# Attention of two blocks first, then the gate and value products of both blocks per weight chunk

## The chip, the cores and the metric

The kernel runs on one core of a Trainium2 chip. The core has a matrix engine (TensorE, PE in the profile; its weight loads are PEld), VectorE (DVE), ScalarE (ACT), GpSimd (POOL) and SyncE (SP), which here only issues transfers. Each engine works through its own instructions in order and waits for the others through semaphores. The metric is the time of one execution on the device in microseconds.

## The reference

Three stages, one behind the other: attention over keys and values averaged in groups of 8, a gated layer (4608 tokens, 512 to 1536 to 512), and a second layer with ELU (512 to 2048 to 512).

```python
k_p = k.reshape(B, H, Sp, pool, D).mean(axis=3)
v_p = v.reshape(B, H, Sp, pool, D).mean(axis=3)
scores = scale * np.matmul(q, k_p.transpose(0, 1, 3, 2))
attn = softmax(scores)                      # 72 keys per head
x = np.matmul(attn, v_p)                    # 8 batches of 576 tokens, 8 heads of 64
gate = 1.0 / (1.0 + np.exp(-(x @ w_gate)))
val = x @ w_val
x = gate * val @ w_out
h = x @ w_in
out = np.where(h > 0.0, h, np.exp(np.minimum(h, 0.0)) - 1.0) @ w_out2
```

The weights arrive as 64-bit floats, two 32-bit words for each number.

## The kernel before, in words

The 4608 tokens are worked in 12 blocks of 384, each of three tiles of 128. A block of 384 tokens may reach over two batches of 576: blocks 0 and 2 lie in one batch, block 1 in two. Every matrix product is made of three passes of single-precision matmuls: each operand is kept as a high part (a copy that ScalarE rounds) and a low part (the difference, on GpSimd or VectorE), and `PASSES` multiplies high by high, high by low and low by high. `split` makes both parts.

**Weights.** The gated layer's hidden size of 1536 is cut in `C1` = 12 chunks of 128. For each chunk three tiles must be converted from 64-bit words: gate, value and output weights, 36 jobs in all. One call of `convert` works on VectorE (L106, L110, L116, L120: clamp, shift and two merges), with a magnitude on ScalarE (L188) one job ahead, and ends with the split of the job before: high part on ScalarE, low part on GpSimd (both by the helper at L93 and L94). The raw words come through two buffers `raw` and, for most even jobs up to job 30, through places of the output weights that are still free; jobs 29 and 31 to 35 go through the two `raw` buffers alone. SyncE issues all loads in program order.

**Attention of a block.** Keys of a batch: five tiles are summed on VectorE (`pool_k`, L354), transposed on TensorE, and copied by ScalarE and VectorE into `kbd` (`emit_k`). Values: `pool_v` (L373, L375) and `place_v` on GpSimd (L384), which fills ten rotating buffers `vbd`. Per tile of queries: `emit_q` transposes, `emit_s` makes the scores (L414) and on VectorE their maximum and difference (L422, L425), `emit_exp` the exponential on ScalarE, `emit_norm` the sums on VectorE (L436 to L438) and the product on GpSimd (L439), `emit_t` the transposes (L454) and their split into `pt`. `emit_pv` multiplies `pt` with the values and splits the result into `x`. One PSUM buffer of two banks, `at`, serves keys, queries, scores, transposes and half of the value products in turn.

**Gated layer of a block.** For each chunk: gate product (12 matmuls, L501, into one of two banks `gv`), sigmoid on ScalarE (L509), value product (12 matmuls), sigmoid times value on VectorE (L513), split into `g`; one chunk later the output product (12 matmuls, L520) adds to four banks `acc`. Behind the last chunk `flush_y` copies these to row tiles and stores them.

**Order.** The order of the program is written out by hand. Ahead of the first chunk, block 0's attention is made and five jobs are converted. In block 0 each chunk holds three calls of `convert`: one between sigmoid and value product, one behind the value product, one behind the split of `g`. Attention of block n+1 is spread over the chunks of block n by `plan`. From block 1 on, `prepare` takes 20 steps per block of the 170 that make the second layer's weights. The second layer starts behind block 11.

Of the kernel before, what the change touches and what calls it, by code (L numbers as in the profile page):

```python
# [24 lines left out]
def fused_kernel(  # L25
# [22 lines left out]

    nc = tc.nc
# [28 lines left out]
    y_dram = [dram.tile([P, KD, NB], F32, name=f"yd{i}", tag=f"yd{i}") for i in range(NBLK)]  # L78
    w_dram = [dram.tile([P, 2, 7, 256], F32, name=f"wd{i}", tag=f"wd{i}") for i in range(C2 // 2)]
# [362 lines left out]
    def emit_t(t, spare=False):  # L442
        n, i = divmod(t, TPB)
        if i == 0:
            pt[n] = at_p.tile([P, 2, NCH, NB], F32R, name="pt", tag="pt")
# [9 lines left out]
        for m, c0, c1, src in (  # L455
# [3 lines left out]
            hi = pt[n][:m, 0, c0:c1, i * P:(i + 1) * P]  # L459
            lo = pt[n][:m, 1, c0:c1, i * P:(i + 1) * P]  # L460
# [5 lines left out]
    def emit_pv(n):  # L466

        p = pt.pop(n)
        x = act.tile([P, 2, KD, NB], F32R, name="x", tag="x")
# [6 lines left out]
        for o, w, b, s in segs(n * NB, NB):  # L476
            for j in range(HP):
                for e in range(2):
                    vb, m = v_bd[b, j, e]
                    for a_w, a_p in PASSES:  # L480
# [3 lines left out]
                            rhs=p[:m, a_p, j + e, o:o + w],  # L484
# [120 lines left out]
    with tc.manual_schedule():  # L605
# [3 lines left out]
        def spare(name):  # L609
            return wts.tile([P, 4, 512], F32, name=name, tag="wg", bufs=C1)  # L610

        k0, q0, qt0, p0, v0, q1, k1, v1 = [
            spare(x) for x in ("k0", "q0", "qt0", "p0", "v0", "q1", "k1", "v1")
        ]
        l0, l1 = [wts.tile([P, 2, 512], F32, name=x, tag="wo", bufs=C1) for x in ("l0", "l1")]
        fetch_to(1)
        load_all("k", 0, k0, l0[:, 0])
        fetch_to(2)
        for i in range(TPB):
            load_q(i, q0[:, i])  # L620
        fetch_to(3)
        load_all("v", 0, v0, l0[:, 1])
        fetch_to(4)
# [14 lines left out]
        convert(1, 1, 0)  # L638
# [3 lines left out]
        open_to(2)  # L642
        for i in range(TPB):
            emit_q(i, qt0[:, i])
        convert(1, 2)
        ph = p0.rearrange("p a n -> p (a n)")
        ph = [ph[:, i * HK:(i + 1) * HK] for i in range(TPB)]
        emit_exp(emit_s(0, ph[0]))
        emit_exp(emit_s(1, ph[1]))
        emit_norm(0, ph[0])  # L650
        convert(1, 2)
        emit_exp(emit_s(2, ph[2]))
        emit_norm(1, ph[1])
        emit_t(0, True)
        for c in range(NCH):
            pool_v(0, c)
        emit_norm(2, ph[2])
        place_v(0, 0)
        place_v(0, 1)
        emit_t(1, True)  # L660
        convert(1, 2)
        place_v(0, 2)
        place_v(0, 3)
        emit_t(2, True)
        for i in range(TPB):
            load_q(TPB + i, q1[:, i])
# [89 lines left out]
        for n in range(NBLK):  # L756
# [3 lines left out]
            for c in range(C1):  # L760
# [16 lines left out]
                elif c in QUIET:  # L777
                    prepare()
# [236 lines left out]
```

## Time and profile before

| | us |
|---|---|
| median of 3 runs | 1940.83 (1938.94 to 1941.63) |
| the profiled execution | 1936.11 |
| its span, first to last instruction | 1934.1 |
| TensorE busy | 1839.1 (95%) |
| VectorE busy | 922.0 (48%) |
| ScalarE busy | 795.1 (41%) |
| GpSimd busy | 510.6 (26%) |

Times within the span count from its first instruction. In a line of the timeline the first number is the start, the second the duration; a part in brackets is the time for which the engine was idle before it and what ended that. `x12` is a number of instructions merged into one line.

### The profile page before, as it was taken

The numbers are of one execution on the slowest core, as the hardware profiler recorded it, in microseconds if no ns is written. First come the engines' busy times: TensorE is split into PE (matmuls) and PEld (weight loads), VectorE is DVE, ScalarE is ACT, GpSimd is POOL, SyncE is SP. The second block draws the span as 40 slices with busy tenths as digits, with TensorE's granted clock in tenths as the row PEclk, the third lists the DMA queues.
The fourth block names the chain that finished last, engine by engine and source line by source line (L and its number), as shares of the span: only waits on it lengthen the run. The fifth ranks groups of instructions, "written<-read, shape, count | busy, mean of one in ns | idle before, by whom it ended". The sixth has DMA issues, their size and how long they took to land.

```text
span 1934.1 us, 25810 instructions
## 1 busy us (share of the span) xinstructions
PE 1839.1 (95%) x9996; PEld 1730.7 (89%) x9996; DVE 922.0 (48%) x1531; ACT 795.1 (41%) x1499; POOL 510.6 (26%) x523
## 2 busy tenths in 40 slices
PE   3776999999999999999999998999999999999999
PEld 3665999999999999999999997898989899999997
DVE  7997455554445554555532133443444344443422
ACT  3543334333333333443333223454454444544543
POOL 4454222222213122223222112222222222222222
PEclk7888999999999999999999999999999999999999
DMA  7332123232223322232310324334353343344330
GB/s 221 110 128 80 50 90 106 76 99 71 85 77 90 128 69 82 96 110 80 104 28 1 137 97 188 117 137 159 120 189 124 125 182 115 145 149 147 153 115 33
DMA packets 115771, 213.49 MB, mean 110 GB/s; under 512 B 43968, under 2 KB 72640, under 8 KB 115648
## 3 DMA queue, kind: packets, MB, share of 16 engines
q1 hardware_dynamic: 115648, 211.84, 32.1%
q8 instruction: 78, 1.28, 0.3%
q14 instruction: 45, 0.37, 0.1%
HBM read 169.87 MB, written 41.94 MB: 110 GB/s over the span
## 4 chain that ended last, share of the span: by engine, by line
PE 85%; DVE 9%; ACT 2%; DMA 2%; issue 1%; POOL 0%; SPq 0%; DVEq 0%; ACTq 0%; POOLq 0%
PE gv L501 27%; PE oacc L896 20%; PE bank L850 18%; PE acc L520 13%; PE xv L481 2%; PE atv L481 2%; PE ats L414 2%; DVE ks L354 2%; DVE nt L106 1%; DVE nt L116 1%; DVE nt L120 1%; PE atq L404 1%; PE att L454 1%; ACT L509 1%; DMA rkv<-in_k_dram 1%
## 5 line engine op out<-in xcount | busy, mean ns | idle before, releaser
L501 PE MATMUL gv<-x,wg 128*128 128x384 f32 x3456 | 654.1, 342 | 22.9 <-DVE sg L513 19.6
L501 PEld LDWEIGHTS gv<-x,wg 128*128 128x128 f32 x3456 | 608.5, 191 | 29.4 <-ACT wo L93 14.1
L896 PE MATMUL oacc<-w2o,gc 128*128 128x512 f32 x1728 | 454.5, 394 | 4.8 <-ACT yo L537 2.4
L896 PEld LDWEIGHTS oacc<-w2o,gc 128*128 128x128 f32 x1728 | 319.9, 188 | 54.5 <-DVE yo L535 3.2
L850 PE MATMUL bank<-form,wr 128*128 128x384 f32 x1728 | 354.0, 339 | 1.9 <-DVE ea L863 1.4
L94 POOL TENSOR_TENSOR g<-sg,g 128x384 fp32r<-128x384 f32 x144 | 156.1, 1084 | 720.6 <-ACT g L93 720.6
L850 PEld LDWEIGHTS bank<-form,wr 128*128 128x128 f32 x1728 | 315.3, 188 | 25.7 <-DVE ea L863 1.7
L520 PE MATMUL acc<-g,wo 128*128 128x384 f32 x1728 | 328.0, 336 | 2.9 <-POOL g L94 2.9
L520 PEld LDWEIGHTS acc<-g,wo 128*128 128x128 f32 x1728 | 302.6, 189 | 6.6 <-POOL g L94 4.5
L513 DVE TENSOR_TENSOR sg<-sg,gv 128x384 f32<-128x384 f32 x144 | 79.2, 550 | 328.0 <-PE gv L501 328.0
L94 POOL TENSOR_TENSOR gc<-ea,gc 128x384 fp32r<-128x384 f32 x96 | 98.1, 1022 | 299.3 <-ACT gc L93 296.2
L94 POOL TENSOR_TENSOR gc<-eb,gc 128x384 fp32r<-128x384 f32 x96 | 98.0, 1020 | 267.3 <-ACT gc L93 245.3
L509 ACT ACTIVATE sg<-gv 128x384 f32<-128x384 f32 x144 | 70.7, 491 | 226.5 <-PE gv L501 226.0
L93 ACT ACTIVATE g<-sg 128x384 fp32r<-128x384 f32 x144 | 75.6, 525 | 176.8 <-DVE sg L513 176.6
L859 ACT ACTIVATE ea<-bank 128x384 f32<-128x384 f32 x48 | 23.6, 492 | 157.6 <-PE bank L850 157.6
L863 DVE SCALAR_TENSOR_TENSOR ea<-ea,bank 128x384 f32<-128x384 f32 x48 | 26.6, 555 | 116.6 <-ACT ea L860 116.6
L94 DVE TENSOR_TENSOR pt<-att,pt 128x512 fp32r<-128x512 f32 x72 | 34.8, 486 | 99.3 <-ACT pt L93 99.2
L859 ACT ACTIVATE eb<-c 128x384 f32<-128x384 f32 x48 | 25.2, 525 | 129.3 <-DVE c L880 129.3
L874 DVE TENSOR_TENSOR u<-p,bank 128x384 f32<-128x384 f32 x48 | 26.6, 555 | 99.0 <-PE bank L850 96.8
L93 ACT ACTIVATE gc<-eb 128x384 fp32r<-128x384 f32 x96 | 50.4, 525 | 56.8 <-DVE eb L863 33.0
L93 ACT ACTIVATE gc<-ea 128x384 fp32r<-128x384 f32 x96 | 50.5, 526 | 55.4 <-DVE ea L863 55.4
L509 ACT ACT_TABLE_LOAD x34 | 43.6, 1283 | 66.5 <-PE gv L501 66.3
(104 smaller groups left out, 1885.3 us busy)
## 6 DMA issues: line engine op xcount, KB each, us to landing
wr<-wd SPq DMA_DIRECT2D x96, 896.0 KB, 6.3
rw<-in_moe_w_out_dram SPq DMA_DIRECT2D x23, 512.0 KB, 3.6
yd<-yo SPq DMA_DIRECT2D x48, 192.0 KB, 2.1
r<-yd SPq DMA_DIRECT2D x24, 384.0 KB, 7.6
out_dram<-po SPq DMA_DIRECT2D x36, 256.0 KB, 2.0
rw<-in_moe_w_in_dram SPq DMA_DIRECT2D x16, 512.0 KB, 4.4
wd<-rw SPq DMA_DIRECT2D x16, 512.0 KB, 3.4
wod<-rw SPq DMA_DIRECT2D x16, 512.0 KB, 2.8
```

Source lines behind the costliest of these rows:

```text
L93: nc.scalar.activation(out=dst_hi, in_=src, func=AF.Copy)
L94: eng.tensor_tensor(out=dst_lo, in0=src, in1=f32(dst_hi), op=ALU.subtract)
L354: nc.vector.tensor_reduce(out=t[:n, 0], in_=r.rearrange("p (r d) -> p d r", r=POOL), op=ALU.add, axis=AX.X)
L414: nc.tensor.matmul(a[o:o + n, j // 2, (j % 2) * w:(j % 2 + 1) * w], lhsT=qt[:, j * P + o:j * P + o + n], rhs=kbd[b % 2][:, j * w:(j + 1) * w],
L481: nc.tensor.matmul(d[j][:, o:o + w], lhsT=vb[:m, a_w].rearrange("p e d -> p (e d)"), rhs=p[:m, a_p, j + e, o:o + w], start=(e == 0 and a_w ...
L501: nc.tensor.matmul(d, lhsT=w[:, i, a_w, j], rhs=x[:, a_x, j], start=(j == 0 and a_w == 0 and a_x == 0), stop=(j == KD - 1 and a_w == 1),)
L509: nc.scalar.activation(out=sg, in_=gps, func=AF.Sigmoid)
L513: nc.vector.tensor_tensor(out=sg, in0=sg, in1=vps, op=ALU.mult)
L520: return lambda: nc.tensor.matmul(acc[m], lhsT=wo[c][:, a_w, m * P:(m + 1) * P], rhs=g[:, a_g], start=(c == 0 and a_w == 0 and a_g == 0), ...
L850: nc.tensor.matmul(bank[b ^ flip], lhsT=wp[q][a_w][:, w, j * P:(j + 1) * P], rhs=form_tile(s, a)[j][:, a_x], start=opens and n == 0, stop= ...
L859: nc.scalar.activation(out=e, in_=src, func=AF.Relu, scale=-1.0)
L896: return lambda: nc.tensor.matmul(acc[t + i], lhsT=g[c][:, a_g, i * P:(i + 1) * P], rhs=wo2[2 * q + e][:, a_w], start=opens and p == 0, st ...
```

## The change

The first two blocks are treated by themselves. The attention of both comes ahead of the first chunk, with the same five conversions between the tiles of block 1. Then one loop over the 12 chunks makes, per chunk, block 0's gate and value products with three conversions, block 0's output product of the chunk before, and the gate and value products of block 1 for the chunk before. Block 1's sigmoid times value is not split but stored to HBM (`g_dram`). Behind the loop block 1's 12 output products are made from these stored tiles, among the attention of block 2. From block 2 on the loop is the one of before, and the steps of `prepare` begin there. The second layer's first two output banks are taken from `gv`, the other four from `acc`.

```diff
+        def keep_g(c):
+            sg = emit_sig(emit_gate(x1, c, 0))
+            vps = emit_gate(x1, c, 1)
+            def rest():
+                nc.vector.tensor_tensor(out=sg, in0=sg, in1=vps, op=ALU.mult)
+                nc.sync.dma_start(out=g_dram[c], in_=sg)
+            return rest
...
+        for c in range(C1):
+            gps = emit_gate(x0, c, 0)
+            sg = emit_sig(gps)
+            if rest:
+                rest()
+            convert(1)
+            vps = emit_gate(x0, c, 1)
+            convert(1)
+            g = emit_g(sg, vps)
+            convert(1)
+            last_y()
+            if c == 0:
+                acc = outputs()
+            pend = (0, acc, g, c)
+            if c > 0:
+                rest = keep_g(c - 1)
+        rest()
+        keep_g(C1 - 1)()
+        do(("ldq", 2 * TPB))
...
+        def second_y(n):
+            nonlocal done, pend
+            for _ in range(n):
+                if done < C1:
+                    g = act.tile([P, 2, NB], F32R, name="g", tag="g", bufs=2)
+                    split(g[:, 0], g[:, 1], g_raw.pop(done))
+                    load_g(done + 2)
+                if pend:
+                    last_y()
+                pend = (1, acc, g, done)
+                done += 1
+        for i in range(TPB):
+            t = 2 * TPB + i
+            do(("q", t))
+            second_y(1)
+            scores = emit_s(t)
+            emit_exp(scores)
+            second_y(1)
+            emit_norm(t, scores)
+            second_y(2)
+            do(("ldq", t + 1))
+            if i == 1:
+                for c in range(3):
+                    do(("lk", 2, c))
+            do(("t", t))
+            if i == 2:
+                for c in range(3, NCH):
+                    do(("lk", 2, c))
+                for c in range(NCH):
+                    do(("pk", 2, c))
+        do(("k", 2))
+        emit_pv(2)
-        for n in range(NBLK):
+        for n in range(2, NBLK):
...
-                            ps.tile([P, DM], F32, name="oacc", tag="acc" if i < 4 else "gv", bufs=4 if i < 4 else 2)
+                            ps.tile([P, DM], F32, name="oacc", tag="gv" if i < 2 else "acc", bufs=2 if i < 2 else 4)
```

The part ahead of the loop:

```diff
+        for t in range(2 * TPB):
+            emit_exp(emit_s(t, ph[t]))
+            if t > 1:
+                emit_t(t - 2, True)
+            between(t)
+            emit_norm(t, ph[t])
+            if t > 2:
+                convert(1, 2)
+        for t in range(2 * TPB - 2, 2 * TPB):
+            emit_t(t, True)
+            convert(1, 2)
+        emit_pv(1)
```

`between` holds block 1's keys and queries (t = 0 and 1), batch 0's values and their placement (2 and 3), and batch 1's values with the first two placements and block 0's value products (4).

TensorE, two chunks in the middle of block 0. Before, a chunk is gate and value products with one weight chunk (`wg_...`), then the output product of the chunk before, with parts of block 1's attention between:

```order
L501 MATMUL gv<-x,wg_826 128x384 x12
L454 MATMUL att<-ident,p 128x128 x4
L454 MATMUL att<-ident,p 64x128
L501 MATMUL gv<-x,wg_826 128x384 x12
L520 MATMUL acc<-g,wo_811 128x384 x12
```

The same two places in the changed kernel; `wg_699` and `wg_767` belong to neighbouring chunks:

```order
L507 MATMUL gv<-x,wg_767 128x384 x24
L526 MATMUL acc<-g,wo_752 128x384 x12
L507 MATMUL gv<-x,wg_699 128x384 x24
L507 MATMUL gv<-x,wg_873 128x384 x24
L526 MATMUL acc<-g,wo_858 128x384 x12
```

A chunk has grown from 36 products to 60, the last 24 of them block 1's with the weights of the chunk before, and no attention stands between them.

VectorE in one chunk of the changed kernel's loop; L519 is block 0's sigmoid times value, L793 block 1's, the groups of four one conversion each:

```order
L519 TENSOR_TENSOR sg<-sg,gv 128x384
L118 SCALAR_TENSOR_TENSOR nt<-rw,nt 128x512
L108 TENSOR_SCALAR nt<-nt 128x512
L122 SCALAR_TENSOR_TENSOR nt<-rw,nt 128x512
L112 TENSOR_SCALAR nt<-nt 128x512
L793 TENSOR_TENSOR sg<-sg,gv 128x384
L118 SCALAR_TENSOR_TENSOR nt<-rwo,nt 128x512
L108 TENSOR_SCALAR nt<-nt 128x512
L122 SCALAR_TENSOR_TENSOR nt<-rwo,nt 128x512
L112 TENSOR_SCALAR nt<-nt 128x512
```

Before, the place of L793 held parts of block 1's attention (key and value sums, scores, probabilities).

SyncE behind the loop, with the loads of the kept products (`rg<-gd`), of queries (`rq`) and of keys (`rkv`):

```order
L319 DMA rq<-in_q_dram 128x8x64
L801 DMA rg<-gd_83 128x384
L801 DMA rg<-gd_84 128x384
L544 DMA yd_71<-yo 128x384 x4
L801 DMA rg<-gd_85 128x384
L801 DMA rg<-gd_86 128x384
L801 DMA rg<-gd_87 128x384
L801 DMA rg<-gd_88 128x384
L319 DMA rq<-in_q_dram 128x8x64
```

All of these but the query loads and the stores of `yo` are new; each query load stands behind the loads of kept products that the program issues before it, and each of those needs one of the two `raw` buffers free.

## Rows read from the trace of the kernel before

**Rows 1.** Page, busy tenths of TensorE in 40 equal slices of the span

```profile
PE   3776999999999999999999998999999999999999
```

**Rows 2.** Windows cut at the first gate product of blocks 0, 1, 2

```profile
core 0: us, PE busy (x) PEld busy (x) DVE busy (x) ACT busy (x) POOL busy (x), PEclk, DMA share, GB/s
0.00:49.40 49.40, 19.88 (x84) 16.01 (x85) 35.73 (x59) 16.64 (x33) 19.71 (x31) 0.79 0.80 223
49.40:201.90 152.50, 107.91 (x535) 97.92 (x534) 127.70 (x180) 68.54 (x116) 72.53 (x60) 0.87 0.30 99
201.90:289.40 87.50, 86.61 (x515) 85.17 (x514) 43.34 (x70) 35.09 (x63) 17.02 (x15) 1.00 0.25 77
```

**Rows 3.** Chain that ended last, one output group of block 1

```profile
276.34 2.08 PE acc L520 x12
```

**Rows 4.** Timeline of VectorE and GpSimd in one chunk of block 0

```profile
85.68 0.54 DVE L513 TENSOR_TENSOR sg<-sg,gv 128x384 f32<-128x384 f32 x1
86.17 1.81 POOL L94 TENSOR_TENSOR wo<-nt,wo 128x512 fp32r<-128x512 f32 x1 [1.63 <-ACT wo L93]
86.75 1.51 DVE L106 TENSOR_SCALAR nt<-nt 128x512 f32<-128x512 f32 x1
...
90.67 0.46 DVE L368 COPY kbd<-atk 64x288 f32<-64x288 f32 x1 [0.66 <-ACT kbd L367]
...
93.57 0.69 DVE L116 SCALAR_TENSOR_TENSOR nt<-rwo,nt 128x512 int32<-128x512 int32 x1
...
96.64 0.55 DVE L513 TENSOR_TENSOR sg<-sg,gv 128x384 f32<-128x384 f32 x1
```

**Rows 5.** Timeline, parts of attention on VectorE and GpSimd

```profile
8.42 3.78 DVE L354 TENSOR_REDUCE ks<-k 128x64 f32<-128x512 f32 x4 [2.45 <-DMA k<-in_k_dram]
...
21.51 0.76 DVE L425 TENSOR_TENSOR p<-ats,mx 128x576 f32<-128x576 f32 x1
22.18 0.74 DVE L436 TENSOR_REDUCE sm<-p 128x8 f32<-128x576 f32 x1
...
30.81 1.02 DVE L373 TENSOR_REDUCE vs<-v 128x64 f32<-128x512 f32 x1
...
79.49 0.69 DVE L94 TENSOR_TENSOR pt<-att,pt 128x512 fp32r<-128x512 f32 x1 [2.61 <-ACT pt L93]
...
195.31 3.47 POOL L384 TENSOR_TENSOR vbd<-vhl,mask 128x256 fp32r<-128x256 f32 x6
```

**Rows 6.** Timeline of VectorE at the last weight tiles

```profile
174.09 0.43 DVE L106 TENSOR_SCALAR nt<-nt 128x512 f32<-128x512 f32 x1 [3.20 <-ACT nt L188]
...
179.62 0.43 DVE L106 TENSOR_SCALAR nt<-nt 128x512 f32<-128x512 f32 x1 [2.03 <-ACT nt L188]
```

**Rows 7.** Transfers by issue (KB, us to landing), then timeline, instructions of a tile

```profile
rq<-in_q_dram SPq DMA_DIRECT2D x1, 256.0 KB, 3.2
rkv<-in_k_dram SPq DMA_DIRECT2D x1, 256.0 KB, 2.6
yd<-yo SPq DMA_DIRECT2D x12, 192.0 KB, 2.0
...
294.56 0.53 ACT L93 ACTIVATE g<-sg 128x384 fp32r<-128x384 f32 x1 [2.19 <-DVE sg L513]
295.16 1.03 POOL L94 TENSOR_TENSOR g<-sg,g 128x384 fp32r<-128x384 f32 x1 [10.25 <-ACT g L93]
300.91 0.69 ACT L431 ACTIVATE p<-p 128x576 f32<-128x576 f32 x1
303.81 1.43 POOL L439 TENSOR_TENSOR p<-p,sm 128x576 f32<-128x576 f32 x1 [0.41 <-DVE sm L438]
```

**Rows 8.** Timeline of TensorE, two gate groups behind waits in block 0

```profile
135.57 3.59 PE L501 MATMUL gv<-x,wg 128*128 128x384 f32 x12 [2.73 <-DVE sg L513]
...
146.66 2.32 PE L501 MATMUL gv<-x,wg 128*128 128x384 f32 x12 [2.02 <-DVE sg L513]
```

**Rows 9.** Timeline at the start of the second layer's outputs

```profile
1175.88 0.96 PE L896 MATMUL oacc<-w2o,gc 128*128 128x512 f32 x3 [2.44 <-ACT yo L537]
...
1184.60 0.47 ACT L872 ACTIVATE p<-bank 128x384 f32<-128x384 f32 x1
```

More of the change, by code (lines that the diff above doesn't have):

```diff
@@ L78, in fused_kernel @@
     y_dram = [dram.tile([P, KD, NB], F32, name=f"yd{i}", tag=f"yd{i}") for i in range(NBLK)]
+    g_dram = [dram.tile([P, NB], F32, name=f"gd{i}", tag=f"gd{i}") for i in range(C1)]
     w_dram = [dram.tile([P, 2, 7, 256], F32, name=f"wd{i}", tag=f"wd{i}") for i in range(C2 // 2)]
@@ L444, in emit_t @@
         if i == 0:
-            pt[n] = at_p.tile([P, 2, NCH, NB], F32R, name="pt", tag="pt")
+            if n == 1:
+                pt[n] = [wts.tile([P, NCH, NB], F32R, name=f"pt1{h}", tag="wg", bufs=C1) for h in range(2)]
+            else:
+                both = at_p.tile([P, 2, NCH, NB], F32R, name="pt", tag="pt")
+                pt[n] = [both[:, h] for h in range(2)]
         p = p_t.pop(t)
@@ L468, in emit_pv @@
         p = pt.pop(n)
-        x = act.tile([P, 2, KD, NB], F32R, name="x", tag="x")
+        pool, tag = (at_p, "pt") if n == 1 else (act, "x")
+        x = pool.tile([P, 2, KD, NB], F32R, name="x", tag=tag)
         a = ps_at.tile([P, 2, 512], F32, name="atv", tag="at")
@@ L755, in fused_kernel, with outputs, last_y @@
         pend = None
-        for n in range(NBLK):
+        def outputs():
+            return [ps.tile([P, NB], F32, name="acc", tag="acc", bufs=4) for _ in range(KD)]
+        def last_y():
+            if pend is not None:
+                pn, pacc, pg, pc = pend
+                emit_y(pacc, pg, pc)
+                if pc == C1 - 1:
+                    flush_y(pn, pacc)
+        def keep_g(c):
[5 more added lines that the diff above has]
+            return rest
@@ new lines, in fused_kernel @@
+        rest()
+        keep_g(C1 - 1)()
+        do(("ldq", 2 * TPB))
+        plan(2)
+        g_raw = {}
+        for c in range(2):
+            load_g(c)
+        last_y()
+        acc = outputs()
+        pend = None
+        done = 0
+        def second_y(n):
[6 more added lines that the diff above has]
+                if pend:
+                    last_y()
+                pend = (1, acc, g, done)
+                done += 1
@@ new lines, in fused_kernel @@
+        for i in range(TPB):
+            t = 2 * TPB + i
[14 more added lines that the diff above has]
+                    do(("lk", 2, c))
+                for c in range(NCH):
+                    do(("pk", 2, c))
@@ L809, in fused_kernel @@
                     emit_pv(n + 1)
-                if pend is not None:
-                    pn, pacc, pg, pc = pend
-                    emit_y(pacc, pg, pc)
-                    if pc == C1 - 1:
-                        flush_y(pn, pacc)
+                last_y()
                 if c == 0:
-                    acc = [ps.tile([P, NB], F32, name="acc", tag="acc", bufs=4) for _ in range(KD)]
+                    acc = outputs()
                 pend = (n, acc, g, c)
```

95 lines of the change are left out of this document (43 added, 52 removed).

## The prediction

> **What bounds the kernel now.** The busy share of TensorE in 40 slices of the span comes first: 9 or more almost everywhere, but 3, 7, 7, 6 in the first four slices [rows 1]. So the change can only win where it works, in the first 290 us. The same stretch cut at the first gate product of each block says how much is there [rows 2]: 49.4 us before block 0's first gate product, 152.5 us for block 0, 87.5 us for block 1, and block 1 is TensorE's own pace (86.61 us busy at a granted clock of 1.00). In block 0 VectorE is busy 127.7 of 152.5 us, TensorE 107.9 at 0.87 of its clock. The timeline of that stretch shows why: each chunk converts three weight tiles on VectorE, and TensorE waits for the product of sigmoid and value, which stands behind these conversions. About 65 us of block 0 over block 1's pace, and most of the first 49.4, are what can be saved. The reader should keep one mark: block 2's first gate product starts at 289.4. From there on both kernels have the same work left, so the whole question is when the changed kernel gets there.
>
> **Stage 1, attention of two blocks.** TensorE has little to do here; VectorE's order sets the pace. Its work, by count and duration [rows 5]: ten key and ten value reductions with the value casts, 21.0 us (five keys 4.7, five values of 1.02 with casts 5.8); six pairs of score maximum and subtraction, 0.76 each and 1.55 a pair, 9.3; six sums with two short instructions behind them, 0.74 and in all about 1.2, 7.2; six low halves of the transposed probabilities, 0.69 and 0.28, 6.0; two key copies 0.9 [rows 4]; five conversions of which the first has half its steps, about 9.7; block 0's four low halves of x, 2.3. That is 56 us. Conflicts with GpSimd (below) add some 4. It starts when the first keys have landed, 8.42 now and about 7.3 then, since the keys are issued ahead of the first weight tile. VectorE also waits: about 4 us from the keys to the first scores as now, 2.2 for the second key transposes, 1.6 for the scores behind them, and 1.4 or so per tile for the high half of the probabilities, which ScalarE writes only behind the exponential that comes after the scores (2.61 in the row shown, with other work around it): 15 in all. 7.3+56+4+15 puts the fifth conversion's end at 83. GpSimd then does the low half of that weight tile and only behind it the six late placements of block 1's values (3.47 for six), which the second half of block 1's value products needs: 88. One more group and a copy of x: block 0's first gate product at **89**, 40 us later than now. If VectorE's waits were all filled it would be 76; if every placement and tile conflicted, 96.
>
> **Stage 2, the paired chunks.** Per chunk TensorE now has five groups of 12 products, 2.08 each [rows 3]: 10.4 us. VectorE keeps its three conversions and one product and gets a second one. A chunk of the present trace has just that: from 85.68 to 96.64 it holds three conversions, the product of 0.54 and a key copy of 0.46 where the second product will stand, and takes 10.96 us [rows 4]. Why so long, when a conversion's four instructions take 2.2 us by themselves (two merges of 0.69, clamp and shift of 0.43 each)? In it the clamp of 0.43 us [rows 6] takes 1.51 while GpSimd writes a low half, and GpSimd's 1.29 becomes 1.81 when VectorE comes first: the two take turns. The product of sigmoid and value, which reads one operand from PSUM, keeps its 0.55. The Trainium skill, GPSIMD Engine Reference, Specifications, says that GpSimd shares its SBUF interfaces with VectorE and contends with VectorE instructions in a two-port mode or with two SBUF inputs; by that rule the free share of VectorE is not free, which speaks against this change, and the trace agrees. By VectorE's durations alone (7.7 us) a chunk would run at TensorE's 10.4, and ten chunks would end 5.5 us sooner; I take the 10.96, since the measured chunk holds the same instructions. TensorE's 10.4 fits just inside, with about 0.5 us waiting per chunk: the second block's sigmoid stands on ScalarE behind the last weight copy of the chunk.
>
> From 89: chunk 0 has no second block and few conflicts, VectorE ends it at 99; chunk 1 at 110; seven chunks of 10.96 to 186. Chunk 9 meets the last weight tiles, which all share two buffers: VectorE waits 3.20 and 2.03 us for them now [rows 6], and will again; these waits hide some conflicts, so 14.7, to 201. Conversions are over then: two chunks at 10.4 and the last pair of groups, 4.2, end at **227**. Storing the kept products costs the chunks nothing: one 192 KB transfer per chunk lands in 2.0 us [rows 7] and its buffer is wanted six or more later; without that cover each would add its landing time.
>
> **Stage 3, block 1's output products beside block 2's attention.** TensorE has 35 us of work here, but the products of one probability tile hang on a chain. SyncE issues the query tile behind the last two loads of kept products, and the second of those waits for GpSimd to free its buffer, which happens near the end of the tile before. A query tile lands 3.2 us after its issue [rows 7], so TensorE stands idle about 2.5 us at each of the three tiles. Then: transposes 0.65, one output group 2.1, scores 1.1, maximum and subtraction 1.6, exponential 0.69, the high half of g 0.53 behind it on ScalarE, its low half 1.03 on GpSimd, an output group 2.1, the normalisation 1.43 and another low half 1.03 against one more group, 2.3 in all, the last group 2.1, transposes 0.7. With the 2.5 that is 15.3. The first tile reaches its end 16 us behind 227 (2.1 of block 0's last outputs, query landed at 4.3, no first group), the second and third at 31 and 47. Block 3's keys come last: the fourth key tile can be loaded only when the first is reduced, its landing takes 2.6, two reductions, a copy, five transposes and the key copies follow; TensorE waits some 8 us and starts block 2's value products at 56. With 4.2 for them and 1.2 for x the gate would start at 61.4.
>
> A bound remains for the clock: a gate group after 2.02 us of waiting took 2.32, one after 2.73 took 3.59 [rows 8]. Three waits of 2.5 and one of 8 cost between 0 and 1.3 us each; I take the 1.3, as 2.5 is nearer to 2.73: 5.2 us. Block 2's first gate product then starts at 227+66.6, or **293.5**, against 289.4: **4.1 us later**.
>
> **Edits that cost nothing.** Six switches of ScalarE's table leave block 0 and its attention leaves the conversions; both are in the stages above. The weight preparation for the second half moves one block later; its 170 steps at 20 per block then end in block 10, beside TensorE's full pace; if block 10 lost it, two or three us. The first two output banks of the second half move from the accumulators to the gate banks. The present trace has waits of 2.44 and less there, but TensorE next needs the copy that ScalarE makes at 1184.60, behind the four stores of the last block [rows 9], and this does not move: 0, at best 4.
>
> **Sum.** 1936.1 of the profiled execution and 4.1 give 1940.2. The median of the runs shown, 1940.83, lies 4.7 above that execution; with it the forecast is **1945 us**, 0.2% slower. About 0.2% (3.9 us) is what a measurement can tell from no change.
>
> **Rivals.**
> *Stage 3 runs without its query waits (faster).* For it: the loads are small, and the queue has nothing else to do. Against: the buffers bind it, not the transfer. If the three query tiles land before they are wanted, 3 times 2.5 and 3 times 1.3 go, 11.4 us: 282, and 1934. It decides from stage 3 at under 58.6 us, 8 below my sum.
> *Stage 1 is shorter (same).* If half of the 15 us of waits on VectorE is filled, 7 us go: 1938. For it: five conversions are spread between the tiles. Against: the present stage 1 has the same waits, although its conversions stand there too.
> *The clock stays low (slower still).* TensorE is about half idle in stages 1 and 3. If in stage 3 two of four output groups per tile run like the 3.59, six groups lose 1.3 more, and the value products and the paired chunks' start another 2: 10 us, 1955. For it: 0.87 mean clock in block 0 at 71% busy. The Trainium skill, TensorE: Matmul & The Clock Gate, Part 1, calls the throttled state the default that activity releases, which by the low busy share of stage 3 would mean this case.
>
> **How the numbers follow.** My sum, with 1941 to 1951 as its own range, 0.45; of that 0.17 lies within 0.2%. Without query waits 0.22, nearly all faster. A short stage 1 0.17, mostly same. A low clock 0.16. So faster 0.24, same 0.31, slower 0.45. Range 1930 to 1958: the bounds of stage 1 (76 to 96) and of the rivals, their ends left out.
>
> **What would show it.** Block 0's first gate product at 85 to 93; the paired chunks 10.7 to 11.2 apart, TensorE waiting for ScalarE's sigmoid or VectorE's product, not for weights, and chunk 9 some 4 longer; the last gate or value group of the second block ending near 227; in stage 3 waits of 2 to 3 us on query tiles and one of 8 on the key copies; block 2 at 293. The forecast is wrong if the chunks run at 10.4, if stage 3 takes under 59 us, or if time appears behind block 2, where I have put none.

## The result and the profile after

| | before | after |
|---|---|---|
| median of 4 runs each, same chip, us | 1941.12 (1938.94 to 1941.63) | 1954.88 (1951.32 to 1955.27) |
| ratio, 95% interval | | 1.0074 [1.0056, 1.0093] |
| profiled execution, us | 1936.11 | 1955.27 |
| its span, us | 1934.1 | 1953.5 |

The changed kernel is 0.74% slower, 13.8 us by the medians. The two profiled executions lie 19.4 us apart in span, because the one of before is 5.0 us below its median and the one of after 0.4 above. The account below is made on the traces, so it has to explain 19.4.

The page of the changed kernel, TensorE's busy tenths and its clock in 40 slices, beside [rows 1]:

```profile
PE   4799769999999999999999997999999999999999
PEclk7699889999999999999999998999999999999999
```

Its windows, cut as in [rows 2] but by the new stages: the attention of two blocks, the paired chunks, block 1's outputs beside block 2's attention.

```profile
core 0: us, PE busy (x) PEld busy (x) DVE busy (x) ACT busy (x) POOL busy (x), PEclk, DMA share, GB/s
0.00:86.68 86.68, 43.81 (x192) 37.10 (x193) 58.01 (x100) 25.45 (x54) 27.27 (x47) 0.73 0.45 128
86.68:230.32 143.64, 131.96 (x710) 129.59 (x709) 103.75 (x150) 54.21 (x100) 63.28 (x44) 0.95 0.35 114
230.32:299.20 68.88, 49.64 (x229) 43.60 (x229) 20.97 (x33) 17.35 (x37) 15.38 (x15) 0.83 0.31 89
```

Of the four low slices of before (3, 7, 7, 6) the first two are still low, and the other two have moved from the third and fourth place to the fifth and sixth. The stages predicted at 89, 138 and 66.6 us took 86.7, 143.6 and 68.9, and block 2's first gate product starts at 299.2: 9.8 us later than before, where 4.1 were forecast. Two more losses lie behind it. The second layer's first product starts at 1175.49 against 1160.85, 14.6 us later, so blocks 2 to 11 lose 4.9 more. The start of the second layer's outputs brings another 4.9: from that first product to the first copy of an output tile it is 139.6 us against 134.7. 9.8, 4.9 and 4.9 are 19.6; from there to the end the two traces agree within 0.2.

**Paired chunks.** TensorE's timeline of the changed kernel:

```profile
86.68 10.98 PE L507 MATMUL gv<-x,wg 128*128 128x384 f32 x48
...
114.06 2.24 PE L526 MATMUL acc<-g,wo 128*128 128x384 f32 x12
...
188.04 2.24 PE L526 MATMUL acc<-g,wo 128*128 128x384 f32 x12
...
193.89 2.38 PE L507 MATMUL gv<-x,wg 128*128 128x384 f32 x12 [1.49 <-DVE sg L519]
202.59 6.89 PE L507 MATMUL gv<-x,wg 128*128 128x384 f32 x24 [6.32 <-ACT sg L515]
209.32 2.24 PE L526 MATMUL acc<-g,wo 128*128 128x384 f32 x12
```

From the output group at 114.06 to that at 188.04 are seven chunks of 10.57 us, close to TensorE's own 10.4. The chunk behind them, with the last weight tiles, takes 21.3. VectorE and GpSimd in one of the seven:

```profile
157.94 0.54 DVE L519 TENSOR_TENSOR sg<-sg,gv 128x384 f32<-128x384 f32 x1
...
159.34 1.78 DVE L122 SCALAR_TENSOR_TENSOR nt<-rwo,nt 128x512 int32<-128x512 int32 x1
161.04 1.24 DVE L112 TENSOR_SCALAR nt<-nt 128x512 int32<-128x512 int32 x1
162.86 0.56 DVE L793 TENSOR_TENSOR sg<-sg,gv 128x384 f32<-128x384 f32 x1 [0.58 <-issue]
...
166.97 1.51 DVE L112 TENSOR_SCALAR nt<-nt 128x512 int32<-128x512 int32 x1
168.41 0.54 DVE L519 TENSOR_TENSOR sg<-sg,gv 128x384 f32<-128x384 f32 x1
...
159.06 1.51 POOL L96 TENSOR_TENSOR wo<-nt,wo 128x512 fp32r<-128x512 f32 x1 [1.32 <-ACT wo L95]
```

The conflicts are there (1.78 for a merge that takes 0.69 alone, 1.24 and 1.51 for a shift of 0.42), but VectorE has only 0.6 us of idle time beside them in this chunk, against some 0.75 in the chunk of [rows 4]. TensorE has no wait at all between the two output groups: it is busy for 73.81 of the 73.98 us, VectorE for 67.21. So TensorE's own pace is the limit of these chunks, and VectorE's order lies close behind it.

ScalarE in the long chunk:

```profile
200.98 0.66 ACT L190 ACTIVATE nt<-rw 128x512 f32<-128x512 f32 x1 [3.78 <-DMA rw<-in_moe_w_out_dram]
...
202.06 0.47 ACT L515 ACTIVATE sg<-gv 128x384 f32<-128x384 f32 x1
```

`convert` opens the magnitude (L190) one tile ahead. The last one waits for its transfer at the head of ScalarE's order; behind it stands block 1's sigmoid, for which TensorE waits 6.32 us. Its next 24 products then take 6.89 us instead of some 4.4; the granted clock is 0.50, the lower level, in the first 4.0 us of them.

The kernel before has the same order at the same tile, ScalarE first, then TensorE:

```profile
184.36 0.66 ACT L188 ACTIVATE nt<-rw 128x512 f32<-128x512 f32 x1 [3.84 <-DMA rw<-in_moe_w_out_dram]
...
185.44 0.47 ACT L509 ACTIVATE sg<-gv 128x384 f32<-128x384 f32 x1
...
177.13 3.94 PE L501 MATMUL gv<-x,wg 128*128 128x384 f32 x12 [8.26 <-DVE sg L513]
...
185.97 0.61 PE L501 MATMUL gv<-x,wg 128*128 128x384 f32 x2 [0.82 <-ACT sg L509]
```

There TensorE waited only 0.82 us for the sigmoid behind the last magnitude, but it had waited 8.26 us a little earlier for VectorE's product, which stands behind conversions that wait for such magnitudes.

**Stage 3.** Waits of TensorE in this stage (total us, times, longest):

```profile
PE atq L406 <- DMA rq<-in_q_dram: 7.0, 3, 2.5
PE atk L366 <- ACT ks L357: 6.1, 5, 3.2
PE acc L526 <- POOL g L96: 2.5, 6, 0.7
PE acc L526 <- ACT g L95: 2.0, 3, 0.8
```

The first two are the predicted waits, three on queries and one string on keys; the other two are on the kept products.

**The start of the second layer's outputs**, ScalarE's timeline (the first three lines) and TensorE's, where [rows 9] had a wait of 2.44 and ScalarE's copy at 1184.60:

```profile
1190.02 0.47 ACT L543 ACTIVATE yo<-acc 128x384 f32<-128x384 f32 x1
1197.35 0.49 ACT L543 ACTIVATE yo<-acc 128x384 f32<-128x384 f32 x1 [6.86 <-DMA yd<-yo]
...
1201.38 0.47 ACT L973 ACTIVATE p<-bank 128x384 f32<-128x384 f32 x1
...
1201.91 2.29 PE L951 MATMUL bank<-form,wr 128*128 128x384 f32 x6 [8.10 <-ACT p L973]
1203.99 2.33 PE L997 MATMUL oacc<-w2o,gc 128*128 128x512 f32 x5
```

Before this TensorE had one wait of 1.57 us; here it waits 8.10 in one piece, because ScalarE's copy waited 6.86 us for the landing of a store. The two groups behind the wait run at a granted clock of 0.50 and take 2.29 and 2.33 us instead of 1.2 to 1.3.

### The profile page after: what moved, and what is told of

Read it like the earlier page. It is cut to its first block, busy times and chain, and to the rows that moved or that the text cites. A ratio compares the mean times of both kernels' runs of the same rounds, so it can differ in the third digit from the quotient of the medians.

```text
span 1953.5 us, 25893 instructions
## 1 busy us (share of the span) xinstructions
PE 1851.2 (95%) x9996; PEld 1742.3 (89%) x9996; DVE 912.5 (47%) x1531; ACT 777.9 (40%) x1489; POOL 508.9 (26%) x523
## 4 chain that ended last, share of the span: by engine, by line
PE 84%; DVE 6%; DMA 4%; ACT 3%; issue 1%; POOL 1%; SPq 0%; ACTq 0%; DVEq 0%; POOLq 0%
PE gv L507 27%; PE oacc L997 20%; PE bank L951 18%; PE acc L526 13%; PE ats L416 2%; PE xv L487 2%; DVE ks L356 2%; PE atv L487 1%; PE atq L406 1%; PE att L460 1%; DMA rkv<-in_k_dram 1%; DMA yd<-yo 1%; DVE vs L375 1%; DMA rkv<-in_v_dram 1%; DMA rwo<-in_moe_w_val_dram 0%
## 5 line engine op out<-in xcount | busy, mean ns | idle before, releaser
L507 PE MATMUL gv<-x,wg 128*128 128x384 f32 x3456 | 644.1, 340 | 11.0 <-ACT sg L515 6.9
L96 POOL TENSOR_TENSOR g<-sg,g 128x384 fp32r<-128x384 f32 x132 | 144.0, 1091 | 676.8 <-ACT g L95 676.8
L519 DVE TENSOR_TENSOR sg<-sg,gv 128x384 f32<-128x384 f32 x132 | 72.6, 550 | 289.1 <-PE gv L507 289.1
L95 ACT ACTIVATE g<-sg 128x384 fp32r<-128x384 f32 x132 | 69.2, 524 | 161.7 <-DVE sg L519 161.7
```

The costliest lines, as they stand in the source:

```text
L95: nc.scalar.activation(out=dst_hi, in_=src, func=AF.Copy)
L96: eng.tensor_tensor(out=dst_lo, in0=src, in1=f32(dst_hi), op=ALU.subtract)
L507: nc.tensor.matmul(d, lhsT=w[:, i, a_w, j], rhs=x[:, a_x, j], start=(j == 0 and a_w == 0 and a_x == 0), stop=(j == KD - 1 and a_w == 1),)
L519: nc.vector.tensor_tensor(out=sg, in0=sg, in1=vps, op=ALU.mult)
```

## The experiments

Each kernel was timed against the kernel before on its own chip; differences between two variants are differences of their ratios times 1940 us, and as each ratio has an interval of some 0.15% to either side, such a difference is good to about 4 us. The single gains below (1.6 to 4.3 us) are at that limit or under it, so what is read from them rests on the traces. The traces place it more finely, but each is one execution. The theory to test: the loss is in orders and shared buffers at five places, not in the pairing itself. The rivals stand with each run.

**a_old_banks.** The second layer's accumulators as before:

```diff
-tag="gv" if i < 2 else "acc", bufs=2 if i < 2 else 4
+tag="acc" if i < 4 else "gv", bufs=4 if i < 4 else 2
```

> The changed kernel, with the six output accumulators of the second layer in the banks of the kernel before (four from acc, then two from gv). If the one long wait of 8.10 us at the start of the second layer's outputs, which is followed by groups at 2.29, 2.33 and 2.10 us, comes from the new assignment of the banks, the time falls by 3 to 5 us against the changed kernel's 1954.9, to some 1950 to 1952, and the wait comes in several pieces again. If the wait comes from a store of the last block's outputs that happened to land 2.4 us late in the one traced execution, the time stays within 1 us of 1955.

Measured: ratio 1.0061 [1.0044, 1.0078], median 1949.98, by the ratios 2.5 us better. TensorE's waits are in pieces again:

```profile
1189.23 0.96 PE L997 MATMUL oacc<-w2o,gc 128*128 128x512 f32 x3 [2.44 <-ACT yo L543]
1191.77 1.65 PE L997 MATMUL oacc<-w2o,gc 128*128 128x512 f32 x3 [1.58 <-DVE yo L541]
```

**b_new_banks.** The kernel before with the new assignment of the banks (the same edit the other way).

> The kernel before, with only the banks of those six accumulators assigned as in the changed kernel. If the assignment costs what the changed kernel's trace shows there, the time rises by 2 to 5 us over the kernel before, to 1943 to 1946, with one wait of some 6 to 8 us ahead of the first outputs. If it was the late store, no change within 1 us.

Measured: 1.0004 [0.9993, 1.0016], 0.8 us, not told from none. But the long wait, and the slow group behind it, came over with the edit:

```profile
1179.19 0.73 PE L896 MATMUL oacc<-w2o,gc 128*128 128x512 f32 x2 [1.85 <-DVE yo L535]
1185.66 2.29 PE L850 MATMUL bank<-form,wr 128*128 128x384 f32 x6 [5.74 <-ACT p L872]
```

So the single wait belongs to the banks, not to chance: in the six traces with the new ones it is there (5.7 to 8.1 us), in the eight with the old ones it is not. Its price is less clear. The timed runs give 2.5 and 0.8 us, neither of them told from none. In the traces the stretch from the second layer's first product to the first copy of an output tile takes 136.9 to 139.6 us with the new banks and 134.5 to 134.7 in seven of the eight with the old, so 2 to 5 us more. With the old banks the same low clock is granted (0.50 from 1180 to 1184 in the kernel before), only earlier and partly under the shorter waits. The eighth, b_late_prep, takes 138.2 with the old banks: there a copy of VectorE ends the waits later (1.92 us of wait for it instead of 0.44 in the kernel before). So lateness at this place costs time without the new banks too, and how much of the 4.9 belongs to each stays open.

**a_magnitude.** In the tenth paired chunk alone the third conversion opens no tile ahead:

```diff
-            convert(1)
+            convert(1, 2, int(c != 9))
             last_y()
```

> The changed kernel, with ScalarE's magnitude of the last weight tile opened one conversion later, in the tenth paired chunk only. If TensorE's wait of 6.32 us there is only ScalarE's order (a magnitude that waits for its transfer, ahead of the second block's sigmoid), the time falls by 5 to 6 us to some 1949, and the chunk takes 15 to 16 us instead of 21.3. If the transfer itself sets the end (the wait only moves to the next conversion), it stays within 1 us of 1955.

Measured: 1.0052 [1.0032, 1.0072], median 1948.01, 4.3 us better by the ratios, under the 5 to 6 that were expected. TensorE:

```profile
187.78 2.24 PE L526 MATMUL acc<-g,wo 128*128 128x384 f32 x12
...
198.30 4.43 PE L507 MATMUL gv<-x,wg 128*128 128x384 f32 x24 [2.19 <-ACT sg L515]
202.58 2.24 PE L526 MATMUL acc<-g,wo 128*128 128x384 f32 x12
```

The chunk takes 14.8 us instead of 21.3, the products behind the shorter wait run at a granted clock of 1.00, and block 2's first gate product starts 6.6 us earlier, at 292.63. The rival falls: the transfer was not the end, the place of the magnitude in ScalarE's order was.

**b_late_prep.** The kernel before, with the preparation of the second layer's weights one block later:

```diff
-                elif c in QUIET:
+                elif n > 1 and c in QUIET:
                     prepare()
...
-                if n > 0:
+                if n > 1:
                     for _ in range(1 + (c in (3, 10))):
                         prepare()
```

> The kernel before, with the preparation of the second layer's weights beginning one block later (block 2 instead of block 1), as it does in the changed kernel, and nothing else. If the 4.8 us that the changed kernel loses inside blocks 3 and 5 come from which steps of the preparation meet which block's attention, the time rises by 4 to 5 us, with block 5 near 91 us instead of 87, less up to 1 us that block 1 gains by having no steps. If they come from something else (the state that the new start leaves behind), no change within 1 us.

Measured: 1.0024 [1.0013, 1.0035], 4.7 us slower, with none of the changed kernel's new stages in it (the interval is 2.5 to 6.8 us). Lengths of blocks 2 to 11, from the first of VectorE's two output copies of one block to that of the next, in us:

```
block            2    3    4    5    6    7    8    9    10   11
before          89.3 90.2 89.3 87.0 89.5 88.0 88.6 89.2 85.1 86.4
after           88.7 91.6 89.3 91.0 88.7 88.4 88.6 89.8 85.2 86.5
b_late_prep     88.7 91.1 89.4 91.3 90.2 88.4 88.6 89.5 85.2 86.4
a_all           88.7 89.6 89.3 91.2 88.2 88.4 89.0 90.0 85.2 86.4
a_all_prep      94.8 89.8 89.2 87.1 89.6 88.1 88.7 90.5 85.0 86.5
a_all2          88.7 91.7 89.3 90.4 88.6 88.5 88.6 91.5 85.1 86.5
a_all2_prep     88.8 91.6 90.6 88.1 91.5 88.1 88.7 91.0 85.0 86.4
```

Single blocks of the same order differ between two executions: blocks 4 and 6 of b_new_banks, which up to the second layer is the kernel before, take 87.7 and 90.5. So differences of 1 to 1.6 us in this table say little, those of block 3 among them. Block 5 stands out of it: it loses some 4 us in both kernels whose preparation starts late. The kernel before, VectorE's score maximum of one tile in block 5 (its scores begin at 590.94), and the transposes of its probabilities:

```profile
592.12 0.76 DVE L422 TENSOR_REDUCE mx<-ats 128x8 f32<-128x576 f32 x1 [0.74 <-PE ats L414]
...
600.25 0.71 PE L454 MATMUL att<-ident,p 128*128 128x128 f32 x5
```

The same tile in the changed kernel (its scores begin at 600.88), with ScalarE's magnitude ahead:

```profile
599.68 0.67 ACT L234 ACTIVATE nt<-rw 128x512 f32<-128x512 f32 x1 [6.51 <-DMA rw<-in_moe_w_in_dram]
...
604.14 0.69 DVE L118 SCALAR_TENSOR_TENSOR nt<-rw,nt 128x512 int32<-128x512 int32 x1
...
605.48 0.74 DVE L424 TENSOR_REDUCE mx<-ats 128x8 f32<-128x576 f32 x1
...
612.19 0.76 PE L460 MATMUL att<-ident,p 128*128 128x128 f32 x5 [1.73 <-POOL p L441]
```

A step's merges (and a value reduction before them) stand ahead of a tile's score maximum, which starts 4.6 us behind the first scores instead of 1.2; the probabilities are normalised later by as much, and TensorE waits at their transposes, as it does nowhere in block 5 of the kernel before. VectorE itself is late there, because the clamp ahead waited 5.75 us for a magnitude that ScalarE could not make before its transfer landed (6.51 us). The block 5 of b_late_prep has such a wait too (7.61 us), that of the kernel before none over 1.3. It looks like the cause found in the tenth chunk again, but no run moved this magnitude by itself, so this is a reading of traces.

**a_query.** Query tiles fetched earlier in stage 3:

```diff
+        do(("ldq", 2 * TPB))
         rest()
         keep_g(C1 - 1)()
-        do(("ldq", 2 * TPB))
...
             do(("q", t))
+            do(("ldq", t + 1))
             second_y(1)
...
             second_y(2)
-            do(("ldq", t + 1))
```

> The changed kernel, with each query tile of the third stage fetched earlier: the first ahead of the last two stores of the kept products, the next ones right behind the transposes of the tile before, instead of behind that tile's four loads of kept products on SP's queue. If the stage's length is set by the queries' waits (2.10, 2.41 and 2.51 us, with half the clock behind them), it falls from 68.9 us to some 58 to 62 and the time by 7 to 11 us, to 1944 to 1948. If the chain of kept products (two buffers, ScalarE's upper halves and GpSimd's lower halves, 0.8 and 0.7 us of wait at an output group) sets it instead, the waits only move there and the time falls by 0 to 3 us.

Measured: 1.0054 [1.0039, 1.007], 3.9 us better, between the two. The waits on transfers are gone, and two of the three are replaced. TensorE at the second tile:

```profile
248.56 0.63 PE L406 MATMUL atq<-ident,rq 128*128 128x128 f32 x4 [2.08 <-issue]
```

The profile names no releaser here. What frees the place is the eviction of the tile before (two copies and two subtractions) out of `at`, the attention's only pair of PSUM banks, into which the transposes also go. That is a third cause, which neither theory had; a run below tests it.

**a_keys.** The key transposes behind the value product of block 2:

```diff
-        do(("k", 2))
         emit_pv(2)
+        do(("k", 2))
```

> The changed kernel, with the next batch's key transposes put behind block 2's value product instead of ahead of it. If TensorE's order is what makes block 2 late there (value product at 292.11, though its weights are split by 284.8), the first gate product of block 2 comes 6 to 8 us earlier, at some 291 to 293 instead of 299.2, and the time falls by 6 to 8 us, to 1947 to 1949. If the keys, summed by 290.4, are needed just as soon behind it, the wait moves behind the value product and the gain is at most 2 us.

Measured: 1.0066 [1.0051, 1.0082], 1.6 us better by the ratios. TensorE:

```profile
285.05 2.35 PE L487 MATMUL atv<-pt,vbd 128*128 128x384 f32 x12 [2.03 <-DVE pt L96]
...
293.25 1.16 PE L366 MATMUL atk<-ident,ks 128*128 128x128 f32 x5 [3.56 <-DVE x L96]
...
296.17 6.37 PE L507 MATMUL gv<-x,wg 128*128 128x384 f32 x24
```

The value product starts 7.1 us earlier than at 292.11, but the first gate product only 3.0 us earlier. The keys need the same pair of banks, and now wait 3.56 us until x is split out of it. The rival is right here.

**a_all.** These four edits together (old banks, later magnitude, earlier queries, later keys).

> The changed kernel with four edits at once: the old banks, the later magnitude, the earlier queries and the later keys. If the four costs lie at places of their own and add (2.5, 6.6, 7 to 11 and 6 to 8 us), the time falls by 20 to 28 us against the changed kernel, to 0.993 to 0.997 of the kernel before, which makes it the faster one. If the third stage's two overlap, by 15 to 18 us, which is between 0.998 and 1.000 of the kernel before.

Measured: 0.9988 [0.9977, 0.9999], median 1937.30, 16.7 us better than the changed kernel and 2.3 better than before. The four single gains by ratio (2.5, 4.3, 3.9, 1.6) make 12.3, which the intervals allow. In the traces block 2's first gate product starts 13.9 us earlier (at 285.29), where the later magnitude, the queries and the keys alone gave 6.6, 5.0 and 3.0. So the gains nearly add; the larger expectation fell because queries and keys gave less each than it had put for them, since they share one pair of banks.

**a_all_prep.** a_all, with every step of the preparation in block 2 doubled, so that the later ones meet the same blocks as before:

```diff
                 if c in QUIET:
-                    prepare()
+                    for _ in range(1 + (n == 2)):
+                        prepare()
...
-                for _ in range(1 + (c in (3, 10))):
+                for _ in range((1 + (c in (3, 10))) * (1 + (n == 2))):
```

> The same four edits, and twice as many steps of the preparation in block 2, so that from block 3 on the same step meets the same block as in the kernel before. If which step meets which block is what costs 4.8 us in blocks 3 and 5, the time falls by a further 3 to 5 us against the four edits alone, less what block 2 pays for its doubled steps; block 5 takes 87 us again. If that loss has another cause, the time rises by what block 2 pays, 0 to 4 us.

Measured: 1.0005 [0.9994, 1.0015], 3.3 us worse than a_all. The table above separates it: block 5 is back at 87.1, as the theory has it, and block 2 pays 6.1. There two steps in a row let ScalarE reach a magnitude before its tile has landed:

```profile
321.99 0.67 ACT L234 ACTIVATE nt<-rw 128x512 f32<-128x512 f32 x1 [5.54 <-DMA rw<-in_moe_w_in_dram]
...
358.51 0.66 ACT L234 ACTIVATE nt<-rw 128x512 f32<-128x512 f32 x1 [7.27 <-DMA rw<-in_moe_w_in_dram]
```

**a_vec.** The changed kernel, with the lower half of block 0's product made by VectorE, to see whether VectorE has time to spare in the paired chunks:

```diff
-            g = emit_g(sg, vps)
+            nc.vector.tensor_tensor(out=sg, in0=sg, in1=vps, op=ALU.mult)
+            g = act.tile([P, 2, NB], F32R, name="g", tag="g", bufs=2)
+            split(g[:, 0], g[:, 1], sg, nc.vector)
```

> The changed kernel, with the lower halves of block 0's product moved from GpSimd to VectorE in the paired chunks (one more instruction of VectorE of some 0.56 us in each of twelve chunks, one less of GpSimd). If TensorE's own work sets the pace of 10.4 to 10.6 us and VectorE has time to spare, the first eight chunks keep it and the time stays within 2 us of the changed kernel. If VectorE still sets the pace there, as it did before, each chunk grows by 0.3 to 0.6 us, and the time by 4 to 7 us, to 1959 to 1962.

Measured: 1.0127 [1.0113, 1.0142], 10.3 us slower than the changed kernel; so both expectations were missed: VectorE has no time to spare for the instruction, and it costs more than the 4 to 7 us of the rival. The output groups of the first chunks stand 11.4 us apart, and TensorE now waits some 0.63 us in each for the sigmoid behind the late conversions; the long tenth chunk grows as well, from 21.3 to 25.0. VectorE, then GpSimd beside it, then VectorE in a chunk without conversions:

```profile
163.20 1.34 DVE L96 TENSOR_TENSOR g<-sg,g 128x384 fp32r<-128x384 f32 x1 [0.94 <-ACT g L95]
...
162.83 1.29 POOL L96 TENSOR_TENSOR wo<-nt,wo 128x512 fp32r<-128x512 f32 x1 [1.31 <-ACT wo L95]
...
221.19 0.56 DVE L96 TENSOR_TENSOR g<-sg,g 128x384 fp32r<-128x384 f32 x1 [0.59 <-ACT g L95]
```

The moved instruction costs not 0.56 but 1.34 us beside GpSimd's low half, and 0.94 of waiting for ScalarE ahead of it, with the rest of the chunk's conversions queued behind both. In the last two chunks, where GpSimd does nothing beside it, the same instruction takes the 0.56. The Trainium skill, GPSIMD Engine Reference, Specifications, has GpSimd contending with VectorE instructions with two SBUF inputs; this one has two, and the trace agrees. So VectorE is no spectator at 10.57: it sets no pace there, since TensorE never waits, but it has only about 1 us a chunk to spare (67.21 us busy in the seven chunks of 73.98), and the moved work takes more.

**a_all_bank.** a_all, with the query transposes of stage 3 in the banks of gate and value, which are idle there:

```diff
+            if 2 * TPB <= t < 3 * TPB:
+                a = ps.tile([P, 512], F32, name="atq", tag="gv", bufs=2)
+            else:
+                a = ps_at.tile([P, 2, 512], F32, name="atq", tag="at")[:, 0, :]
-            a = ps_at.tile([P, 2, 512], F32, name="atq", tag="at")[:, 0, :]
```

> The four edits at once, and the query transposes of the third stage into the banks of gate and value, which nothing uses there, instead of the attention's single pair. If the wait of 2.08 us ahead of the second and third tile is the eviction of the tile before out of that pair, both disappear, and with them some of the half clock: 4 to 7 us less than the four edits alone, to 0.995 to 0.997 of the kernel before. If the chain of kept products behind it sets the pace of a tile, the waits of 0.8 and 0.7 us grow instead and the time falls by 0 to 1 us.

Measured: 0.9963 [0.9949, 0.9977], 4.9 us better than a_all, as the first expectation has it. TensorE at the second tile:

```profile
241.61 0.60 PE L409 MATMUL atq<-ident,rq 128*128 128x128 f32 x4
```

The 2.08 us without a releaser are gone at both tiles, and the waits on the kept products there have not grown (0.53 and 0.63 us, against 0.81 and 0.64 in a_all). That settles the cause left open in a_query.

**a_all2.** a_all_bank, with the key transposes behind block 2's first gate product:

```diff
-        do(("k", 2))
...
             early, pre, mid, post = plan(n + 1)
+            if n == 2:
+                mid[0].insert(0, ("k", 2))
```

> The same as the one with the banks, and the next batch's key transposes not between block 2's value product and its first gate product, but behind that gate product. If the 4.17 us that TensorE waits there for the pair of banks keeps block 2 back, its first gate product comes 2.5 to 3.5 us earlier and the time falls by as much again. If the last split of x sets that start (the query transposes ahead of the gate product wait for the same pair), it falls by 0 to 1 us.

Measured: 0.9953 [0.994, 0.9965], median 1930.32: 9.1 us faster than before. The 1.9 that it is better than a_all_bank lie between the two expectations, and within what two runs can tell. Stage 3 takes 53.7 us (223.13 to 276.80, cut as above) at a clock of 0.92, against 68.9 at 0.83 in the changed kernel and 55.5 in a_all_bank. What is left there is the last split of x:

```profile
276.03 1.11 PE L409 MATMUL atq<-ident,rq 128*128 128x128 f32 x4 [2.83 <-DVE x L96]
276.80 4.19 PE L510 MATMUL gv<-x,wg 128*128 128x384 f32 x12
```

**a_all2_prep.** a_all2, with the missing twenty steps spread, one at a time, over blocks 2 to 5:

```diff
-                if c in QUIET:
+                if c in QUIET or n < 5 or (n == 5 and c < 3):
```

> The version with the banks and the keys behind the gate product, and the twenty missing steps of the preparation given back one by one, six in each of blocks 2 to 4 and two in block 5, each at a place of its own between gate and value product, instead of doubled in block 2. If which step meets which block is the loss of 4 us in block 5 and single extra steps are hidden by TensorE's work, block 5 takes 87 us, blocks 2 to 4 stay within 1 us, and the time falls by 3 to 4 us against the version without them, to 0.993 to 0.994 of the kernel before. If each extra step delays the attention that shares VectorE's and ScalarE's order with it, blocks 2 to 4 pay 3 to 6 us and nothing is won.

Measured: 0.9953 [0.9936, 0.997], the same as a_all2. Block 5 falls from 90.4 to 88.1, but blocks 4 and 6 rise by 1.3 and 2.9. The loss seems to move to other meetings (the 1.3 alone is within the scatter of a block); nothing is won, as the rival has it, though most of the loss is not in the blocks 2 to 4 that it named.

## Why the prediction came out as it did

The sign was right, and so was the first half of the mechanism: block 2 is reached later. The other half was not foreseen. Of the 19.4 us between the traces 9.6 lie behind block 2's start, where the prediction put none and called time there a sign of being wrong. The size was too small, 4 us instead of 13.8, outside the sum's own range of 1941 to 1951; only the range of all rivals, 1930 to 1958, holds it. It is luck that the rival of a low clock names 1955, the time measured: its 10 us are six more slow output groups in stage 3, slow value products and a slow start of the paired chunks. Stage 3 ended 2.3 us above its sum, with three slow output groups in all (4.21, 3.64 and 3.62 us); the rest of the loss lies in chunk 9 and behind block 2. The steps one by one:

1. *Stage 1, 89 us.* 86.7. The sum of VectorE's instructions held (its printed terms give 82.3 for the fifth conversion's end, not 83).
2. *Paired chunks at 10.96.* 10.57, so the step is over-sized by 0.39 a chunk, 2.7 us in seven. The conflicts came, but VectorE's work in a chunk takes 9.6 us on average (67.21 in seven), where the chunk taken as a model had 10.21 busy. The limit was named wrongly: VectorE was to set the pace and TensorE to wait some 0.5 us a chunk, but TensorE has no wait in the seven, so the pace is its own. a_vec shows how close it was: about 1 us more of VectorE's time, and VectorE sets the pace.
3. *"Chunk 9 ... 14.7."* This step failed: 21.3. It carried VectorE's two waits over from [rows 6] and did not ask what else stands in ScalarE's order behind the magnitude that waits. In the kernel before a sigmoid stands behind that magnitude too, but TensorE came to it late and waited 0.82 us; its long wait there, 8.26 us, was for VectorE's product, and [rows 6], which show VectorE's waits, don't hold it. Now there is a second sigmoid per chunk, and TensorE is at it early. With the magnitude moved (a_magnitude) the chunk takes 14.8, close to the step's 14.7.
4. *The end of the loop at 227.* 230.3, from the three differences above (2.3 and 2.7 us less, 6.6 more) and 1.7 us in the first chunks and the last.
5. *Stage 3, 66.6 us.* 68.9, mechanism and size near: query waits of 2.10 to 2.51, output groups of 3.6 to 4.2 behind them, keys last. The terms listed for a tile add to 17.4 with the query wait, not to 15.3; one output group is left out of the sum without a word. The trace bears that out: the group at 256.32 runs beside VectorE's maximum and the exponential, and the second and third tile take 16.9 and 17.1 us, against 15.3 and 1.3 for the clock. TensorE's waits of 0.8 and 0.7 on a tile's kept products are the chain that the terms describe. The faster rival, a stage without query waits, named too few causes: taking away the transfers' lateness (a_query) only uncovers the single pair of banks. Only both together, with the later keys (a_all_bank), give what that rival priced: a stage of 55.5 us, against its 55.2.
6. *The weight preparation, one block later, under "Edits that cost nothing".* This step failed: 4.7 us, shown alone by b_late_prep. I asked whether 170 steps fit into the blocks that are left, and not which attention each would stand in front of on VectorE, or which magnitude would come ahead of its transfer.
7. *"The first two output banks ... 0, at best 4."* Nothing was gained, and the traces have a loss. It rightly saw that ScalarE's copy behind the last stores ends the wait. It missed that outputs which start early leave all the waiting for that copy in one piece, with nothing left to run in it; 2 to 5 us by the traces, while the timed runs (0.8 and 2.5) don't tell it from none.

The edits in a_all gain 16.7 us, more than the 13.8 that the changed kernel had lost, and a_all2 shows that pairing two blocks over the conversions, with the places around it put in order, is 9 us faster than the kernel before. Not all of that need belong to the pairing: the kernel before has the same magnitudes ahead of their transfers at the last weight tiles, and it was not run with them later. Block 5 is 3 to 5 us longer in every version that starts the preparation late and gives it no extra steps; neither placing of the steps that was tried removes this without paying elsewhere.

## What to carry to other kernels

When a change gives an engine's result a new reader, walk the order of the engine that makes it and look for look-ahead work that waits on a transfer: it now holds the reader too. Read the waits of the engine that matters at such a place, and not only those of the engine that you follow. When work is shifted against a periodic pattern, cost the new meetings, not only the sum. And before a wait is taken away, ask what single buffer would end the same idle time a moment later.

## What was not expected of the hardware

The length of a wait did not tell its price in clock. In the tenth chunk of a_magnitude TensorE waited 2.19 us and went on at a granted clock of 1.00 (198.30 to 202.58). In stage 3 of the changed kernel it waited 2.41 us for a query at 251.29, and from there to 255.12 the granted clock was 0.64, so that an output group took 3.64 us instead of 2.1. Ahead of the first, TensorE had run at 1.00 from 187.78 on, with one wait of 1.61; stage 3 has TensorE busy for 49.6 of 68.9 us.

VectorE's price for sharing with GpSimd hangs on the instruction: the product of sigmoid and value kept its 0.54 to 0.56 us in every chunk, the low half that a_vec moved took 1.34, and 0.56 where GpSimd had nothing to do.
